# Totals of three groups interleaved with the next scores, and one more spatial unit as split products, in a retention and gated-MLP kernel

## The chip, the cores and the metric

The kernel runs on one core of a Trainium2 chip. The metric is device time in microseconds (us) of one execution, the median of several runs. The engines are TensorE (PE, with its weight loads as PEld), VectorE (DVE), ScalarE (ACT), GpSimd (POOL) and SyncE (SP), whose queue issues most loads.

## The reference

Retention with 4 batches, 8 heads, 768 positions and head size 64, then a gated MLP on its output:

```
state = gamma * state + k[t] (outer) v[t];  y[t] = scale * q[t] @ state      # per head
h = relu(x @ w_in);  u, v = halves of h                                      # x = y, 512 wide
v_n = (v - mean) / sqrt(var + 1e-6)
out = (u * (w_spatial @ v_n + b_spatial)) @ w_out
```

All inputs and the output are f32; w_spatial is 768 x 768, u and v are 512 wide.

## The kernel before

**Retention.** The sequence is cut into groups of 128 positions, six to a batch (24 groups g), each of two chunks i of 64 positions. For a chunk, 4 pairs of heads hp by 2 heads r are 64x64 matmuls. `place(hp, r)` names the half of the partitions on which head r of pair hp lies, so a matmul uses one quadrant of the 128x128 array: its rows are the half of its operands, its columns the half of its output. An f32 matmul stands as two records in the trace. For each group there are scores (k by q, tile `s`, masked by DVE into `scores`), a sum of k by v, and products with values and states (tile `x`), which give the output of the group.

**Two ways of the k by v sum.** In the steps S (`ret_set`), from group 6 on, scores of the next group and the k by v products of this one (tile `d`) are issued alternately, the latter into the opposite half of the output, and DVE (or ACT, line 369) brings them back to the right half while it adds the old state. In the opening, groups 0 to 5, `total_sum` (word t) adds the products into one standing PSUM tile `total`, and `total_copy` (word k, on ACT) copies it to the state; the next t waits for that copy.

**The MLP.** x is split in a high and a low part (`xh`, `xl`: words h and l after the evict E); v products (word V), u products (word u) and out products (word o) are fp32r products of three terms: high by high, high by low, low by high. A spatial unit (column block j, half of the positions) is `spatial_products`: six f32 products, or, where the half is the second and column j was split by `norm_split` (D), eighteen fp32r ones, with the spatial weights that `split_spatial` (W0 and W1) put in high and low parts by an ACT cast and a DVE residue for each of three blocks. A split column takes two of the four buffers tagged "ca", which the weight splits use before.

**The order.** The strings START, FIRST, REST and LAST are the program order, a word an action. In START every engine keeps that order. In FIRST and later PE keeps it, and other engines are ordered by a planner, but for W's casts and residues, which keep the program order too. In START the words c, H, R split w_in and w_out: c0, c1, c2 on DVE, H a cast on ACT, R the residue on POOL (R1 to R5) or DVE. p22 to p26 scale the values of groups 2 to 6 on ACT by eight multiplications each; j is the mask on DVE, q a block of scores, y01 the second chunk's x products of group 0. In FIRST, I4 is two blocks of u products, the spatial unit of column 0, second half, its gate, and an out product.

The lines that set the buffers:

```python
total[0] = ps_o.tile([P, NP, D], F32, tag="o", name="total")       # one tile for the whole run
return mpool.tile([P, 2, HC, P], dtype, tag="ca", name=name, bufs=4)
return ps_r.tile([P, 2, NP, C], F32, tag="ret", name=name)          # bufs=2: scores and d
```

Of the kernel before, what the change touches and what calls it, by code (L numbers as in the profile page):

```python
# [21 lines left out]


START = (
# [10 lines left out]
)  # L35
FIRST = (
    "S6 W0 I4 W1 D1 X6 J9 S7 G9 D2 I5 X7 J10 G10 D3 W2 S8 W3 I6 X8 S9 V0 G11 W4 I7 X9 J11 S10 "
    "G12 O7 N0 X10 W5 V1 V2 V3 N1 N2 J12 G13 S11 X11 J13 G14 V4 N3 S12 N4 V5 W6 N5"
)
REST = (  # L40
# [21 lines left out]
def tile_retention_gmlp(  # L62
# [12 lines left out]
    nc = tc.nc  # L75
    P = 128
    B = out.shape[0]
# [12 lines left out]
    ROWS = [slice(0, D), slice(D, P)]  # L90
# [27 lines left out]
    def keep(ins):  # L118

        if fixed:  # L120
            tc.keep_in_program_order(ins)

    def mm(out, lhs, rhs, start, stop, pin=False, shared=False):
        ins = nc.tensor.matmul(out, lhs, rhs, start=start, stop=stop, skip_group_check=shared)  # L124
        if pin or pinned or fixed:
            tc.keep_in_program_order(ins)
# [32 lines left out]
    def slot(n, dtype, name):  # L159

        cols = HALF // 2 if dtype == I64 else HALF
        return mpool.tile([P, HC, cols], dtype, tag=f"sp{n}", name=name, bufs=1)
# [5 lines left out]
    for n in ROOMS:  # L168
        t = slot(n, F32, f"room{n}").rearrange("p s c -> p (s c)")
# [85 lines left out]
    def place(hp, r):  # L255

        return ROWS[(r + hp) % 2]
# [40 lines left out]
    total = {}  # L298
    marks = {}

    def total_sum(g, i):
        if not total:
            total[0] = ps_o.tile([P, NP, D], F32, tag="o", name="total")
        for hp in range(NP):
            for r in range(2):
                rows = place(hp, r)
                mm(
                    total[0][rows, hp],
                    naturals[g][rows, i, hp],
                    values[g][rows, i, hp],  # L310
                    start=(g == 0 and i == 0 and hp == 0),
                    stop=True,
                    shared=True,
                )

    def total_copy(g, i):
        dst = states[g][:, 1] if i == 0 else states[g + 1][:, 0]
        keep(nc.scalar.copy(dst, total[0]))

    def score(g, i, hp, r, pin=False):  # L320
        rows = place(hp, r)
        ops = keys[g][rows, i, hp], queries[g][rows, i, hp]
        mm(marks[g][rows, i, hp], *ops, start=True, stop=True, pin=pin)

    def bank(name):
        return ps_r.tile([P, 2, NP, C], F32, tag="ret", name=name)
# [8 lines left out]
    def ret_mask(g):  # L335
        mk = mask_t[:, :].unsqueeze(1).broadcast_to([P, 2 * NP, C])
        s, d = (t.rearrange("p i h c -> p (i h) c") for t in (marks.pop(g), scores[g]))
        keep(nc.vector.tensor_tensor(d, s, mk, ALU.mult))
# [360 lines left out]
    def decay_copy():  # L699
# [17 lines left out]
        "q": lambda b, g, n: ret_scores(n),  # L717
        "p": lambda b, g, n: scale_values(n % 10, pick(n // 10)),
        "j": lambda b, g, n: ret_mask(n),
        "t": lambda b, g, n: total_sum(n // 10, n % 10),  # L720
        "k": lambda b, g, n: total_copy(n // 10, n % 10),
        "y": lambda b, g, n: out_products(n // 10, n % 10),
        "E": lambda b, g, n: out_evict(n),
# [114 lines left out]
```

## Time and profile before

| | |
|---|---|
| median of 3 runs | 373.97 us (372.93 to 374.14) |
| the profiled execution | 374.42 us, span 372.7 us |
| PE busy | 362.0 us (97%) |
| DVE, ACT, POOL busy | 237.2, 155.1, 135.5 us |
| granted TensorE clock | 1.00 |

The span is the time from the first to the last instruction of the profiled execution; its device time is 1.7 us longer. PE's matmuls are pipelined, so a busy PE need not be at its peak.

### The profile page before, as it was taken

How to read it: one execution, taken by the hardware profiler on the slowest of the kernel's cores; microseconds unless marked ns; L12 is line 12 of the kernel's file. 1: busy time of each engine (PE TensorE's matmuls, PEld its weight loads, DVE VectorE, ACT ScalarE, POOL GpSimd, SP SyncE). 2: the span in 40 equal slices, each digit the busy share in tenths (PEclk: the TensorE clock that was granted, in tenths of full speed). 3: DMA queues.
4: the chain of work that ended last, by engine and by line, in shares of the span. 5: the costliest groups of instructions: out<-in, count | busy, mean ns of one | idle time of the engine just before them, and what ended most of it. 6: DMA issues, size and time to landing. Idle time of an engine off the chain costs nothing.

```text
span 372.7 us, 10303 instructions
## 1 busy us (share of the span) xinstructions
PE 362.0 (97%) x4420; PEld 316.6 (85%) x4420; DVE 237.2 (64%) x514; ACT 155.1 (42%) x309; POOL 135.5 (36%) x137
## 2 busy tenths in 40 slices
PE   7798999999999999999999999999999999999995
PEld 3687785797998879999998888999998888999984
DVE  4989979995887866677674543376774433165530
ACT  3595781274334545533114445432323445432232
POOL 2254750001353523526424451327424341325041
PEclk9999999999999999999999999999999999999999
DMA  7997773001331731113305332021404002000022
GB/s 262 413 365 261 272 300 130 0 2 63 138 114 58 253 115 64 61 55 112 118 2 199 114 114 86 8 106 52 179 1 141 3 2 86 0 0 2 0 87 84
DMA packets 13153, 41.20 MB, mean 111 GB/s; under 512 B 1586, under 2 KB 1842, under 8 KB 13108
## 3 DMA queue, kind: packets, MB, share of 16 engines
q1 hardware_dynamic: 12964, 40.42, 29.8%
q8 instruction: 35, 0.57, 0.7%
q10 hardware_dynamic: 144, 0.13, 0.1%
q14 instruction: 10, 0.08, 0.1%
HBM read 34.25 MB, written 6.29 MB: 109 GB/s over the span
## 4 chain that ended last, share of the span: by engine, by line
PE 94%; DMA 2%; DVE 1%; issue 1%; ACT 0%; SPq 0%; POOL 0%; POOLq 0%; DVEq 0%
PE u L124 18%; PE v L124 18%; PE o L124 18%; PE y L124 10%; PE sp L124 8%; PE x L124 7%; PE z L124 5%; PE s L124 3%; PE d L124 3%; PE w L124 3%; DMA decay_t<-in_decay_dram 2%; PE total L124 1%; PE o_last L124 0%; SPq L129 0%; DVE xf L417 0%
## 5 line engine op out<-in xcount | busy, mean ns | idle before, releaser
L124 PE MATMUL u<-xh,winu_w 128*128 128x384 f32 x256 | 68.1, 338 | 0.0
L124 PE MATMUL v<-winv_w,xh 128*128 128x512 f32 x192 | 60.6, 397 | 0.0
L124 PE MATMUL o<-wout_w,gh 128*128 128x512 f32 (+1 forms) x192 | 60.4, 396 | 0.0
L124 PEld LDWEIGHTS u<-xh,winu_w 128*128 128x128 f32 x256 | 46.5, 188 | 0.8
L132 POOL TENSOR_TENSOR xl<-xf,xh 128x512 fp32r<-128x512 f32 x21 | 29.4, 1398 | 37.3 <-ACT xh L434 37.3
L124 PE MATMUL u<-xl,winu_w 128*128 128x384 f32 x128 | 42.9, 335 | 0.0
L124 PEld LDWEIGHTS v<-winv_w,xh 128*128 128x128 f32 x192 | 35.2, 188 | 7.8
L124 PE MATMUL y<-sp,a 128*128 128x384 f32 x216 | 41.6, 336 | 0.0
L124 PEld LDWEIGHTS o<-wout_w,gh 128*128 128x128 f32 x192 | 35.2, 188 | 7.3
L532 ACT CAST a<-vn 128x384 fp32r<-128x384 f32 x42 | 21.6, 514 | 46.0 <-PE y L124 16.9
L132 DVE TENSOR_TENSOR a<-vn,a 128x384 fp32r<-128x384 f32 x42 | 24.9, 593 | 24.6 <-ACT a L532 24.2
L132 POOL TENSOR_TENSOR gl<-ur,gh 128x384 fp32r<-128x384 f32 x24 | 26.8, 1116 | 37.4 <-ACT gh L628 37.0
L124 PEld LDWEIGHTS y<-sp,a 128*128 128x128 f32 x216 | 38.0, 188 | 0.2
L124 PE MATMUL v<-winv_w,xl 128*128 128x512 f32 x96 | 37.5, 390 | 0.0
L124 PE MATMUL o<-wout_w,gl 128*128 128x512 f32 (+1 forms) x96 | 37.3, 389 | 0.0
L475 DVE BATCH_NORM_STATS2 bst<-vr 128x6 f32<-128x512 f32 x24 | 16.6, 691 | 28.6 <-ACT vr L468 28.6
L417 DVE SCALAR_TENSOR_TENSOR xf<-x,decay_t,qd_t 128x128 f32<-128x128 f32 x96 | 27.1, 343 | 10.3 <-PE x L124 9.7
L482 POOL TENSOR_TENSOR rs<-rs,mhalf 128x1 f32<-128x1 f32 x24 | 13.5, 566 | 42.6 <-DVE rs L477 42.1
L124 PE MATMUL s<-qk 64*64 64x64 f32 x768 | 27.4, 221 | 0.1
L124 PEld LDWEIGHTS s<-qk 64*64 64x64 f32 x768 | 25.2, 137 | 2.1 <-issue 1.1
L498 ACT ACTIVATE vn<-vr,nb,rs 128x512 f32<-128x512 f32 x24 | 19.4, 814 | 17.8 <-DVE nb L487 16.8
L593 ACT ACTIVATE ur<-u 128x384 f32<-128x384 f32 x32 | 15.7, 490 | 26.8 <-PE u L124 26.6
(111 smaller groups left out, 671.7 us busy)
## 6 DMA issues: line engine op xcount, KB each, us to landing
qk<-in_groups_dram SPq DMA_DIRECT2D x24, 512.0 KB, 5.4
vk<-in_groups_dram SPq DMA_DIRECT2D x21, 512.0 KB, 4.8
out_dram<-ot SPq DMA_DIRECT2D x23, 256.0 KB, 2.9
wst<-in_w_sp_dram SPq DMA_DIRECT2D x4, 576.0 KB, 7.9
raw<-in_w_inv_dram SPq DMA_DIRECT2D x4, 512.0 KB, 7.3
raw<-in_w_inu_dram SPq DMA_DIRECT2D x4, 512.0 KB, 7.0
raw<-in_w_out_dram SPq DMA_DIRECT2D x4, 512.0 KB, 5.2
third<-in_groups_dram SPq DMA_DIRECT2D x3, 512.0 KB, 7.4
```

The costliest lines, as they stand in the source:

```text
L124: ins = nc.tensor.matmul(out, lhs, rhs, start=start, stop=stop, skip_group_check=shared)
L132: return eng.tensor_tensor(out, whole, high.bitcast(F32), ALU.subtract)
L417: nc.vector.scalar_tensor_tensor(xf[:, hp], t[hp % 2][:, hp // 2].rearrange("p i c -> p (i c)"), qg_t[:, c, hp : hp + 1], qd_t[:, hp], ALU ...
L475: keep(nc.vector.bn_stats(st, norm[b, c][0]))
L482: keep(nc.gpsimd.tensor_tensor(rs, rs, mhalf, ALU.pow))
L498: keep(nc.scalar.activation(vn[b][:, c], v, AF.Identity, bias=nb, scale=rs))
L532: nc.scalar.copy(t[:, 0], whole)
L593: keep(nc.scalar.activation(u, pu[:, :HALF], AF.Relu))
```

## The change

Three parts. In `total_sum` every product goes to the opposite half of the output, and for groups 2, 3 and 4 (words t120 to t141) each is issued right after a score product of the next group; the words q3, q4 and q5 are gone, and the masks j4 and j5 stand later, behind the second half of those scores. `total_copy` copies two halves instead of one whole, swapping them. In FIRST, W1 and a new D0 stand before I4, so that the spatial unit of column 0, second half, takes the split products.

```diff
 START, the parts that differ (before, after):
-... l0 H1 q3 t20 k20 E1 G4 R1 V00 j2 h1 t21 l11 p23 k21 y20 y21 L5 R2 j3 q4 t30 E2 a3 h2 j4 c30 V10 p24 ...
+... l0 H1 t120 k20 E1 G4 R1 V00 j2 h1 t121 l11 p23 k21 y20 y21 L5 R2 j3 t130 E2 a3 h2 c30 V10 p24 ...
-... V20 a5 k30 y30 c32 t31 H3 k31 c50 G5 y31 q5 E3 t40 a4 j5 R3 V21 V12 k40 c40 L6 c51 y40 p25 y41 t41 h3 ...
+... V20 a5 k30 y30 c32 t131 j4 H3 k31 c50 G5 y31 E3 t140 a4 R3 V21 V12 k40 c40 L6 c51 y40 p25 y41 t141 j5 h3 ...
 FIRST:
-    "S6 W0 I4 W1 D1 X6 J9 ...
+    "S6 W0 W1 D0 I4 D1 X6 J9 ...
-    def total_sum(g, i):
+    def total_sum(g, i, with_scores=False):
         if not total:
             total[0] = ps_o.tile([P, NP, D], F32, tag="o", name="total")
+        if with_scores and i == 0:
+            marks[g + 1] = bank(f"s{g + 1}")
         for hp in range(NP):
             for r in range(2):
-                rows = place(hp, r)
+                if with_scores:
+                    score(g + 1, i, hp, r)
+                rows, other = place(hp, r), place(hp, 1 - r)
                 mm(
-                    total[0][rows, hp],
+                    total[0][other, hp],
                     naturals[g][rows, i, hp],
                     values[g][rows, i, hp],
...
     def total_copy(g, i):
         dst = states[g][:, 1] if i == 0 else states[g + 1][:, 0]
-        keep(nc.scalar.copy(dst, total[0]))
+        for r in range(2):
+            keep(nc.scalar.copy(dst[ROWS[r]], total[0][ROWS[1 - r]]))
...
-        "t": lambda b, g, n: total_sum(n // 10, n % 10),
+        "t": lambda b, g, n: total_sum(n // 10 % 10, n % 10, n >= 100),
```

## Rows read from the trace of the kernel before

**Rows 1.** The page, busy us (share of the span) and instructions of PE.

```profile
PE 362.0 (97%) x4420; PEld 316.6 (85%) x4420; DVE 237.2 (64%) x514; ACT 155.1 (42%) x309; POOL 135.5 (36%) x137
```

**Rows 2.** Waits of PE, whole run: who waited for whom, total us, times, longest.

```profile
PE x L124 <- issue: 1.3, 2, 0.9
PE total L124 <- issue: 1.2, 1, 1.2
PE x L124 <- DVE ws L372: 0.2, 1, 0.2
```

**Rows 3.** Busy by stretch: length, busy us (instructions) by engine, clock, DMA share, GB/s.

```profile
16.90:27.40 10.50, 10.50 (x256) 9.17 (x252) 8.93 (x20) 9.81 (x34) 5.47 (x4) 1.00 0.99 370
22.80:41.15 18.35, 16.77 (x398) 14.08 (x392) 17.95 (x36) 13.24 (x39) 9.49 (x7) 1.00 0.77 267
```

**Rows 4.** Timeline of PE, merged: start us, length us, what, count.

```profile
17.48 1.97 PE L124 MATMUL s<-qk 64*64 64x64 f32 x62
...
19.35 0.63 PE L124 MATMUL total<-third 64*64 64x64 f32 x15
...
91.92 0.24 PE L124 MATMUL d<-vk 64*64 64x64 f32 x2
...
92.80 0.23 PE L124 MATMUL d<-vk 64*64 64x64 f32 x2
```

**Rows 5.** The chain that ended last, the two kinds of spatial unit.

```profile
85.27 3.87 PE sp L124 x12
...
95.34 3.12 PE sp L124 x18
```

**Rows 6.** Timeline of ACT: copies and the instruction behind them.

```profile
18.83 0.35 ACT L318 COPY third<-total 128x256 f32<-128x256 f32 x1
19.09 0.62 ACT L205 CAST winv_w<-df 128x512 fp32r<-128x512 f32 x1
...
81.17 0.74 ACT L369 COPY ws<-d 64x256 f32<-64x256 f32 x2
...
81.94 0.52 ACT L244 CAST sp<-wst 128x384 fp32r<-128x384 f32 x1
```

**Rows 7.** Timelines of POOL (R3) and DVE (c50, E3, c40, E5).

```profile
28.09 1.59 POOL L132 TENSOR_TENSOR df<-df,winv_w 128x512 f32<-128x512 f32 x1 [2.67 <-ACT winv_w L205]
29.76 1.33 POOL L212 TENSOR_TENSOR winv_w<-df,room 128x512 fp32r<-128x512 f32 x1
...
28.46 1.50 DVE L182 TENSOR_SCALAR room<-room 128x512 f32<-128x512 f32 x1
30.00 1.37 DVE L184 TENSOR_SCALAR room<-room 128x512 int32<-128x512 int32 x1
31.29 1.11 DVE L417 SCALAR_TENSOR_TENSOR xf<-x,decay_t,qd_t 128x128 f32<-128x128 f32 x4
...
33.37 0.43 DVE L184 TENSOR_SCALAR room<-room 128x512 int32<-128x512 int32 x1
...
41.47 1.12 DVE L417 SCALAR_TENSOR_TENSOR xf<-x,decay_t,qd_t 128x128 f32<-128x128 f32 x4 [0.32 <-PE x L124]
```

**Rows 8.** Busy by stretch from the start to two gaps; the page's instruction queue.

```profile
0.00:16.74 16.74, 11.78 (x223) 7.25 (x223) 11.08 (x23) 6.35 (x11) 4.93 (x14) 1.00 0.89 330
...
0.00:30.70 30.70, 25.66 (x603) 19.46 (x604) 23.40 (x45) 17.73 (x47) 12.94 (x20) 1.00 0.89 331
...
q8 instruction: 35, 0.57, 0.7%
```

**Rows 9.** Timelines of ACT (k50) and PE (y51, V30).

```profile
39.50 0.36 ACT L318 COPY third<-total 128x256 f32<-128x256 f32 x1
...
40.61 0.27 PE L124 MATMUL x<-third,third 64*64 64x64 f32 x3
...
41.28 0.73 PE L124 MATMUL v<-winv_w,xh 128*128 128x512 f32 x2
```

**Rows 10.** Timeline of DVE, the residues of W0.

```profile
84.45 1.49 DVE L132 TENSOR_TENSOR sp<-wst,sp 128x384 fp32r<-128x384 f32 x3
```

More of the change, by code (lines that the diff above doesn't have):

```diff
@@ L24 @@
 START = (
[10 rows of a table removed]
[10 rows of a table added]
 )
 FIRST = (
-    "S6 W0 I4 W1 D1 X6 J9 S7 G9 D2 I5 X7 J10 G10 D3 W2 S8 W3 I6 X8 S9 V0 G11 W4 I7 X9 J11 S10 "
+    "S6 W0 W1 D0 I4 D1 X6 J9 S7 G9 D2 I5 X7 J10 G10 D3 W2 S8 W3 I6 X8 S9 V0 G11 W4 I7 X9 J11 S10 "
     "G12 O7 N0 X10 W5 V1 V2 V3 N1 N2 J12 G13 S11 X11 J13 G14 V4 N3 S12 N4 V5 W6 N5"
```

20 rows, old and new, of the table START are left out of this document.

## Prediction, made before the changed kernel was run

> **What bounds the kernel now.** I read the page first. TensorE (PE) is busy 362.0 of 372.7 us [rows 1]: whatever shortens or delays it late in the run shows one for one. Then the waits of PE over the whole run. One of them, of 0.2 us behind DVE, comes after the first 41 us; the others fall before. Two of the early ones are named "issue", which is time in which PE waited for nothing that the profile shows [rows 2]. So a change after 41 us is worth its PE time; a change before must be traced to what PE waits for. Third, the busy time by stretch. From 16.90 to 27.40 us ScalarE (ACT) works 9.81 of 10.50 us, and from 22.80 to 41.15 us VectorE (DVE) works 17.95 of 18.35 us [rows 3]. PE only looks full there: the two engines that feed it have next to no room.
>
> **The change part by part.**
>
> *1. Scores and totals alternate (t120 to t141).* Before, a block of scores, or of totals, used only two of the four quadrants. The 62 score records at 17.48 took 1.97 us from first start to last end; less the 0.22 us of one record that is 28.7 ns each. Totals: (0.63 - 0.22) / 14 = 29 ns [rows 4]. The later steps S already alternate scores with products that write the opposite quadrant: from the first d pair at 91.92 to the last at 92.80 there are 15 steps of four records, 14.7 ns a record [rows 4]. Three groups have 32 score and 32 total records each: 192 x 14.0 ns = 2.7 us of PE. Its bounds are 0 (alternating does not pay here) and 2.7 us.
>
> The Trainium skill, TensorEngine Tiling, section Restrictions and Gotchas, says that different row tiles cannot use the same PSUM bank at the same time. By it the two score quadrants, which share a bank, would exclude each other, and the alternation would gain nothing. The 14.7 ns rows, same pattern and same banks, speak against it.
>
> *2. What this moves.* The scores of groups 3, 4 and 5 no longer run ahead of their totals. A total waits for its scaled values and for the copy of the total before it (it adds into the bank that the copy reads), and the scores now stand behind that wait on PE. So the 0.9 us that a score block used to cover such waits is gone: t120 waits for p22, t130 for p23 and k21, all on ACT. The masks j4 and j5 go behind c32 and c51 on DVE, with the same work.
>
> *3. The copy of the total is cut in two (k, 11 times).* Source and destination halves are swapped, so one 128x256 copy becomes two 64x256 ones. A whole copy let the next instruction start 0.26 us later (18.83 to 19.09). The nearest rows to a half copy are those of L369, the same form: two begin at 81.17 and the next instruction at 81.94, 0.385 us each with no overlap [rows 6]. A pair therefore costs 0.77 us, 0.50 us more than before. If half copies overlapped as the whole ones do, it would be 0.26 more. Four of them (k11, k20, k21, k30) lie between 16.9 and 27.4 us: 4 x 0.50 = 2.0 us, less the 0.69 us that ACT was idle there [rows 3] = 1.3 us; by the low price 1.04 - 0.69 = 0.35 us. I take the high price, since the row is of the same shape. So H3, the ACT cast behind k30, ends 0.35 to 1.3 us later.
>
> *4. Who waits for H3.* The residue R3 on GpSimd (POOL) starts on it at 28.09, and its two operations run to 31.09. In that time DVE's c50 needed 1.50 and 1.37 us for what takes 0.43 us undisturbed; E3 follows at 31.29 [rows 7]. With R3 late, E3 comes late by 0 to 1.3 us: 0 if c50 slips in ahead of, or between, R3's two operations, and all of it if c50 is held again. From E3 on DVE has no idle time until E5, which waited 0.32 us for PE [rows 7]; masks and splits are as many as before. E4 releases h4, H4, r2 and then k50 on ACT (39.50), now a pair, and k50 releases y51 and so V30 at 41.28 [rows 9]. Before, PE came to y51 at 40.61 us, after k50 had ended [rows 9]; PE, 2 us earlier by the alternation, will now wait for it. With E4 unmoved, the pair ends at 39.50 + 0.77 = 40.27, y51 takes 0.5 us, the turn to V30 0.25 us: V30 at 41.05 instead of 41.28, a gain of 0.23 us. With E4 later by 1.3 us: a loss of 1.1 us. I take the middle, slightly to the bad side, a loss of 0.5 us in START. The 2.7 us of PE then turn into waits at t120, t130 and y51.
>
> *5. The "issue" gaps.* One of 1.2 us stood in the middle of t40, after 603 matmuls; another after 223 [rows 2, 8]. The PE instructions (4420 + 4420, [rows 1]) over the 35 packets of the instruction queue [rows 8] make 253 a packet, 126 matmuls with their loads; the gaps lie 380 = 3 x 127 apart. So I read them as the instruction stream arriving late while the DMA engines are full. The instructions are the same in number, and the reordering puts the boundary 16 pairs further on, behind six V products that take 1.4 us. The gap may shrink from 1.2 to 0. I count it at nothing, because the DVE chain of part 4 ends after it.
>
> The Trainium skill, Runtime: NRT & Kernel Launch, section Instruction fetch mechanics, calls the cost of crossing a 16 KiB boundary mostly hidden. The 1.2 us gap disagrees, if it is one.
>
> *6. FIRST: column 0, second half.* 12 records of an f32 spatial unit took 3.87 us on the chain, the 18 of a split one 3.12 us [rows 5]: -0.75 us, on a PE with no idle time. To have it in time, D0 and W1 must be done early. D0 takes the pair of rooms, and the place on ACT and DVE, that D1 had, and D1 takes D2's; D2 now waits until the unit has read column 0, with some 15 us left. W1's three casts fit into ACT's idle time. Its three DVE residues come behind W0's, which ended at 84.45 + 1.49 = 85.94 [rows 10]: at 86.43, 86.93 and 87.43. The unit starts at 85.10 and needs them, at 0.52 us per pair of weights, at 86.84, 87.36 and 87.89. It fits with 0.4 us to spare. If another 0.95 us DVE operation goes between, the stall is 0.55 us. Bounds: 0.2 to 0.75 us; I take 0.75, since nothing ahead of them grows.
>
> **Sum.** The profiled execution took 374.42 us (span 372.7 and 1.7 around it), 0.45 above the median of the runs, 373.97. 374.42 + 0.5 - 0.75 = 374.2; against the median, **373.7 us**, within what a measurement of this kernel can tell from no change (0.3%, 1.1 us).
>
> **Rivals.**
>
> *PE sets START after all.* c50 or c51 escapes GpSimd (each hold is worth about 1 us on DVE), the half copies overlap, and the gap of part 5 closes. Then START gains 1.2 to 2.7 us, with part 6 1.9 to 3.4: 370.5 to 372.0. For it: holds on DVE depend on shifts of tenths. Against it: ACT's 9.81 of 10.50 us.
>
> *The copies win.* The k pairs put every scaling (p22 to p24) and cast behind them, by 0.5 us each. R3 and the later residue l3 are late and meet other DVE operations that they hold for one more us; START then loses 2 to 2.5 us, after part 6 1.3 to 1.8: 375.2 to 375.8. It decides from about 1.9 us of loss in START. For it: the DVE holds of rows 7; against it: only 2.0 us are added in the tight stretch, less 0.69 of idle.
>
> *Alternation does not pay for totals.* Scores and totals keep 28.7 ns, ACT is as in part 3: a loss of 1.3 us less 0.75: 374.5.
>
> *W1 late:* the 0.75 shrinks to 0.2: 374.3.
>
> **Numbers.** Forecast (START hidden under ACT and DVE, within 1.1 us) 0.48; PE sets START 0.29; copies win 0.15; no alternation 0.04; W1 late 0.04. Faster by over 0.3%: the second, and a little of the first: 0.32. Slower: the third, and a little of the rest: 0.17. Same: 0.51. The range reaches into both main rivals: 371.6 to 375.2. The likeliest case's own range is 372.9 to 374.9.
>
> **What would show it.** Part 1: 32 records of s and total in about 0.5 us. Part 3: the copies of the total in pairs 0.38 apart, ACT with hardly a gap from 17 to 28 us. Part 4: new PE waits at t120, t130 and y51, E3 and E4 between 0 and 1.3 us later. Part 6: 18 records of the split kind in 3.12 us where 12 stood, no wait before them. The prediction is wrong if V30 starts earlier than about 40.3 us or later than 42.8 us, or if the unit of column 0 waits for a residue.

## The result, and the profile after

The change made the kernel slower: 376.99 us (median of 6 runs, 376.61 to 377.75) against 373.98 (6 runs), a ratio of 1.0081, 95% interval 1.0060 to 1.0102. The forecast was 373.7, its range ended at 375.2. The profiled execution took 376.77 us, span 375.0 against 372.7.

The page first, its busy line of all engines and the row of TensorE's granted clock in forty slices:

```profile
PE 362.4 (97%) x4426; PEld 317.1 (85%) x4426; DVE 238.1 (63%) x515; ACT 161.4 (43%) x321; POOL 135.2 (36%) x137
...
PEclk9888999999999999999999999999999999999999
```

PE is 0.4 us busier than before [rows 1] and idle for 12.6 us instead of 10.7. That the alternation and the split products need less of its time does not show in its busy time, partly because the records of two stretches at a lower clock (below) are longer. ACT has 6.3 us more [rows 1] in 12 more instructions: eleven pairs of half copies by 0.50 are 5.5, and the cast of D0 is 0.83. The waits of PE, whole run (who waited for whom, total, times, longest), say where the idle time went [rows 2]:

```profile
PE total L124 <- issue: 3.1, 1, 3.1
PE total L124 <- ACT ws L323: 2.0, 2, 1.7
```

The timeline of PE places them (start, length, what, count, idle time before and its releaser):

```profile
15.80 0.51 PE L124 MATMUL total<-vk 64*64 64x64 f32 x10 [3.13 <-issue]
...
25.47 0.27 PE L124 MATMUL total<-vk 64*64 64x64 f32 x1 [1.66 <-ACT ws L323]
...
43.94 0.73 PE L124 MATMUL v<-winv_w,xh 128*128 128x512 f32 x2
...
87.84 3.70 PE L124 MATMUL sp<-sp,vn 128*128 128x384 f32 x18
```

The first row is t10. At 15.80 it starts when the pair k01 has ended (14.96 + 0.74), not for nothing as the name "issue" says. It waited for k01 before, too: at 14.07 the view names GpSimd's scaling, but that had ended at 13.18, and the whole copy k01 at 13.97. PE (t10), ACT (k01) and GpSimd before:

```profile
14.07 0.68 PE L124 MATMUL total<-vk 64*64 64x64 f32 x16 [1.54 <-POOL vk L296]
...
13.60 0.37 ACT L318 COPY ws<-total 128x256 f32<-128x256 f32 x1
...
12.14 1.04 POOL L296 TENSOR_TENSOR vk<-vk,decay_t 128x512 f32<-128x512 f32 x1 [2.78 <-DMA vk<-in_groups_dram]
```

The second row is t130, behind the pair k21 (24.67 + 0.74). The third is V30, 2.66 us later than before [rows 9]; the fourth the spatial unit of column 0.

**The span in four parts.** From V30 to that unit nothing depends on the change: 43.82 us before, 43.90 after, and 43.8 to 44.0 in the profile of every kernel below. From the group products x of X6, behind the unit and its out products, to the end it is 281.4 to 282.0 in all but one. So each span is the start of V30 + 43.9 + the stretch from the unit to X6 + 281.6. Before: 41.28 + 43.82 + 6.05 + 281.55 = 372.7. After: 43.94 + 43.90 + 5.70 + 281.46 = 375.0. START lost 2.66 us where a loss of 0.5 was forecast; FIRST gained 0.35 where 0.75 was.

ACT's timeline after shows p22, k21, H3 and k50 [rows 6, 9]:

```profile
17.72 2.02 ACT L293 ACTIVATE third<-third,decay_t 128x64 f32<-128x64 f32 x8
...
24.67 0.74 ACT L323 COPY ws<-total 64x256 f32<-64x256 f32 x2
...
30.00 0.62 ACT L205 CAST winv_w<-df 128x512 fp32r<-128x512 f32 x1
...
42.63 0.76 ACT L323 COPY third<-total 64x256 f32<-64x256 f32 x2
```

H3 is 2.61 us late; before it was:

```profile
27.39 0.62 ACT L205 CAST winv_w<-df 128x512 fp32r<-128x512 f32 x1
```

It adds up: p22 starts 0.81 us late (16.91 before); from p22 to H3 ACT is busy 11.88 of 12.28 us against 9.80 of 10.48, so 2.08 more work, of which idle time took only 0.28: 0.81 + 2.08 - 0.28 = 2.61.

DVE's timeline, first c20 and E0, then j4, c50, E3 and E4 [rows 7], then the residues [rows 10]:

```profile
11.56 0.43 DVE L182 TENSOR_SCALAR room<-room 128x512 f32<-128x512 f32 x1 [1.01 <-ACT room L176]
12.02 1.22 DVE L184 TENSOR_SCALAR room<-room 128x512 int32<-128x512 int32 x1
13.17 1.11 DVE L422 SCALAR_TENSOR_TENSOR xf<-x,decay_t,qd_t 128x128 f32<-128x128 f32 x4
...
32.54 0.69 DVE L343 TENSOR_TENSOR ws<-s,mask_t 128x512 f32<-128x512 f32 x1 [2.48 <-PE total L124]
33.15 0.47 DVE L182 TENSOR_SCALAR room<-room 128x512 f32<-128x512 f32 x1
33.65 0.43 DVE L184 TENSOR_SCALAR room<-room 128x512 int32<-128x512 int32 x1
33.99 1.12 DVE L422 SCALAR_TENSOR_TENSOR xf<-x,decay_t,qd_t 128x128 f32<-128x128 f32 x4
...
39.81 1.12 DVE L422 SCALAR_TENSOR_TENSOR xf<-x,decay_t,qd_t 128x128 f32<-128x128 f32 x4
...
87.10 2.42 DVE L132 TENSOR_TENSOR sp<-wst,sp 128x384 fp32r<-128x384 f32 x5
89.44 0.95 DVE L132 TENSOR_TENSOR vn<-vn,vn 128x768 fp32r<-128x768 f32 x1
90.31 0.55 DVE L132 TENSOR_TENSOR sp<-wst,sp 128x384 fp32r<-128x384 f32 x1
```

Three things are to be seen. At 12.02 an operation of c20 takes 1.22 us instead of 0.43 (11.58 to 12.01 before), while GpSimd scales group 1 from 11.92 to 12.96; before, c20 was done when that scaling began, at 12.14. At 32.54 DVE, which from 22.80 to 41.15 us had 0.4 us of idle time before [rows 3], waits 2.48 us: the mask j4 now stands behind t131, and c50 and E3 behind j4. E3 is 2.70 us late, and all of START's loss lies ahead of it. Not all of that is the mask's: E3 reads the products y31, which end on PE at 32.95 (row below) and ended at 29.28 before. So PE alone would have made E3 some 1.7 us late, and j4 and c50 ahead of it add 1.0. At 89.44 the residue of another column (D1) has slipped in ahead of W1's last. The end of y31 on PE:

```profile
32.65 0.30 PE L124 MATMUL x<-qk,ws 64*64 64x64 f32 x8
```

### The profile page after: what moved, and what is told of

It is laid out like the page before. It is cut to its first block, busy times and chain, and to the rows that moved or that the text cites. A ratio compares the mean times of both kernels' runs of the same rounds, so it can differ in the third digit from the quotient of the medians.

```text
span 375.0 us, 10330 instructions
## 1 busy us (share of the span) xinstructions
PE 362.4 (97%) x4426; PEld 317.1 (85%) x4426; DVE 238.1 (63%) x515; ACT 161.4 (43%) x321; POOL 135.2 (36%) x137
## 4 chain that ended last, share of the span: by engine, by line
PE 79%; DVE 10%; DMA 4%; issue 2%; ACT 2%; SPq 1%; POOL 0%; DVEq 0%; ACTq 0%
PE o L124 16%; PE v L124 15%; PE u L124 15%; PE y L124 10%; PE x L124 6%; PE z L124 5%; DMA vk<-in_groups_dram 4%; PE sp L124 3%; PE d L124 3%; PE w L124 2%; PE s L124 2%; DVE df L193 1%; SPq L129 1%; DVE df L132 1%; DVE room L202 1%
## 5 line engine op out<-in xcount | busy, mean ns | idle before, releaser
L124 PE MATMUL v<-winv_w,xh 128*128 128x512 f32 x192 | 61.7, 403 | 0.0
L132 DVE TENSOR_TENSOR a<-vn,a 128x384 fp32r<-128x384 f32 x42 | 25.9, 618 | 24.6 <-ACT a L537 24.2
L537 ACT CAST a<-vn 128x384 fp32r<-128x384 f32 x42 | 21.6, 514 | 46.1 <-PE y L124 16.9
L124 PE MATMUL s<-qk 64*64 64x64 f32 x768 | 28.9, 222 | 0.2 <-DMA qk<-in_groups_dram 0.2
L296 POOL TENSOR_TENSOR vk<-vk,decay_t 128x512 f32<-128x512 f32 x18 | 19.9, 1105 | 18.8 <-DMA vk<-in_groups_dram 10.8
```

The lines of the kernel that those rows point to most:

```text
L132: return eng.tensor_tensor(out, whole, high.bitcast(F32), ALU.subtract)
L296: tc.keep_in_program_order(engine.tensor_tensor(values[g], values[g], vd, ALU.mult))
L537: nc.scalar.copy(t[:, 0], whole)
```

## The experiments

V30 is the start in the profile (41.28 before); the ratio, with its 95% interval, is to runs of the kernel before on the same chip. One per cent is 3.7 us. Each kernel does all of the computation; e4 repeats some scores besides.

| kernel | V30 | time | ratio | interval |
|---|---|---|---|---|
| e1_first_only | 39.50 | 373.67 | 0.9975 | 0.9955 to 0.9996 |
| e2_halves_only | 42.98 | 375.20 | 1.0020 | 0.9997 to 1.0042 |
| e3_start_only | 43.88 | 376.66 | 1.0058 | 1.0038 to 1.0078 |
| e4_fill_second | 45.70 | 381.10 | 1.0174 | 1.0143 to 1.0205 |
| e5_order_only | 41.91 | 376.03 | 1.0035 | 1.0013 to 1.0057 |
| e6_halves_early | 41.65 | 375.92 | 1.0033 | 1.0013 to 1.0053 |
| e7_halves_mid | 41.30 | 373.67 | 0.9991 | 0.9972 to 1.0009 |
| e8_first_d1_late | 41.00 | 374.20 | 1.0000 | 0.9982 to 1.0017 |
| e9_c50_first | 41.77 | 375.77 | 1.0043 | 1.0015 to 1.0072 |
| e10_c50_dve | 43.24 | 375.41 | 1.0033 | 1.0018 to 1.0048 |
| e11_c50_dve_first | 42.93 | 375.76 | 1.0027 | 1.0004 to 1.0049 |
| e12_q4_back | 42.78 | 376.24 | 1.0042 | 1.0018 to 1.0067 |
| e13_order_c50 | 41.64 | 375.28 | 1.0023 | 1.0007 to 1.0039 |
| e14_early_k01 | 40.04 | 375.12 | 1.0018 | 0.9996 to 1.0039 |
| e15_first_pinned | 40.67 | 373.81 | 0.9989 | 0.9972 to 1.0006 |
| e16_all_mends | 41.94 | 374.28 | 0.9994 | 0.9970 to 1.0018 |
| e17_mends_q5 | 41.45 | 373.80 | 0.9984 | 0.9964 to 1.0005 |
| e18_k01_pinned | 40.61 | 374.07 | 1.0008 | 0.9988 to 1.0027 |

V30 and the time don't rank alike, because one profile is one execution: e1, e8, e15 and the kernel before have the same START, and V30 at 39.50, 41.00, 40.67 and 41.28. Sizes are therefore taken from the ratios, mechanisms from the profiles.

**The parts by themselves, and the clock.** The first theory was TensorE's clock: the changed kernel has two stretches below full speed. Its windows, whose columns are as in [rows 3]:

```profile
16.50:20.50 4.00, 4.00 (x108) 3.73 (x99) 3.90 (x10) 3.89 (x13) 0.00 (x0) 0.57 0.80 280
26.80:30.20 3.40, 3.40 (x10) 2.62 (x9) 3.16 (x6) 3.34 (x12) 0.13 (x1) 0.50 1.02 406
```

Before, both stretches had 1.00. In FIRST alone START is that of before; in the halves alone the totals go to the opposite half and are copied in halves, with order and FIRST of before; in START alone FIRST is that of before; the fourth kernel is the change with group 4's scores computed three times over (extra work on PE ahead of t130, to keep it busy).

```diff
 e1, on the kernel before:
-    "S6 W0 I4 W1 D1 X6 J9
+    "S6 W0 W1 D0 I4 D1 X6 J9
 e2, on the kernel before:
-                    total[0][rows, hp],
+                    total[0][other, hp],
...
-        keep(nc.scalar.copy(dst, total[0]))
+        for r in range(2):
+            keep(nc.scalar.copy(dst[ROWS[r]], total[0][ROWS[1 - r]]))
 e3, on the change:
-    "S6 W0 W1 D0 I4 D1 X6 J9
+    "S6 W0 I4 W1 D1 X6 J9
 e4, on the change (A42: the scores of group 4, twice):
-... R2 j3 t130 E2 ...
+... R2 j3 A42 t130 E2 ...
```

> Only the FIRST part of the change (W1 and D0 ahead of I4); START is that of before. Theory (the loss is made in START): 0.35 us below before if a residue of the second weight block comes late behind the residue of column 1, as in the changed kernel; 0.75 us if it is in time. Rival (the loss is made in FIRST, where the DVE work was pulled together): above before, by up to 2 us.

> Only the totals in the opposite half and the copy in two halves; START keeps the blocks of scores q3 to q5, nothing alternates, FIRST is that of before. Theory (a wait at t130 lets the granted clock fall, and the V products behind it run at half speed): the scores of group 4 stand between y21 and t30 and shorten the wait, the clock stays at 1.00 in the V products, and the loss is 0.5 to 1.2 us against before. Rival (the longer copies on ACT alone hold START back, whatever the clock): about 2.5 us above before.

> The whole START part of the change, FIRST as before. Theory and its rival on ACT alone: 2.6 to 2.8 us above before, with the clock at half in two stretches of the first 30 us. Rival (the loss is made in FIRST): within 0.5 us of before.

> The changed kernel with 1.9 us of idle repeats of the scores of group 4 on PE ahead of t130, in the place of its wait. Theory (the clock): the granted clock of V10 to V02 is 1.00, they take 3.3 instead of 5.2 us, and the time is 1.5 to 1.9 us below the changed kernel, about 375.2. Rival (ACT alone): the V products are faster, but what follows waits for ACT and DVE all the same, and the time is within 0.4 us of the changed kernel, 377.

The loss is START's: 0.58% (2.2 us) with FIRST as before. The halves alone, at 1.0020, can't be told from 1. The low clock of the second stretch isn't needed for the loss: in START alone that stretch has full clock,

```profile
26.80:30.20 3.40, 3.40 (x46) 2.60 (x48) 3.14 (x6) 3.34 (x12) 0.11 (x1) 1.00 0.99 398
```

and V30 is at 43.88, as after. t131 comes earlier there, j4 at 30.93 instead of 32.54, but then R3 on GpSimd (30.68) catches c50 and holds one of its operations for 1.40 us: E3 at 33.59 instead of 33.99. Here PE is not what holds E3, since y31 ends at 31.34; the other 2.25 us are c50, behind j4 and beside R3. DVE, then R3's second operation, then y31:

```profile
30.93 0.69 DVE L343 TENSOR_TENSOR ws<-s,mask_t 128x512 f32<-128x512 f32 x1 [0.88 <-PE total L124]
...
32.27 1.40 DVE L184 TENSOR_SCALAR room<-room 128x512 int32<-128x512 int32 x1
33.59 1.11 DVE L422 SCALAR_TENSOR_TENSOR xf<-x,decay_t,qd_t 128x128 f32<-128x128 f32 x4
...
32.02 1.35 POOL L212 TENSOR_TENSOR winv_w<-df,room 128x512 fp32r<-128x512 f32 x1
...
31.04 0.30 PE L124 MATMUL x<-qk,ws 64*64 64x64 f32 x8
```

The fill proved nothing by itself: the extra scores met a gap of their own, 1.96 us put down to "issue", the clock fell all the same (0.64), and j4 came at 33.90.

This does not rule out the clock altogether. The first stretch is below full speed in START alone, too (0.67), and over many runs the time goes with the clock: of 138 runs of the kernel before that stand beside these experiments, the 81 with a mean granted clock of 0.997 or more had a median of 374.01 us, the 43 from 0.993 to 0.996 had 374.73, and the 14 below that 375.76. The change's six runs had 0.988 to 0.994. So the clock may make a part of the loss. It does not make all of it: at like clocks and on the same chip, the order alone (e5, below) took 375.01 against 374.10 us (6 and 18 runs at 0.997 or more), and the early half copies (e6) 375.99 against 374.52 (11 and 13 runs from 0.993 to 0.996).

**Order, early copies and middle copies apart.** Each on the kernel before, with totals in their old quadrants: the order of START alone, whole copies; then the first three copies in halves (k00, k01, k10); then the four of the prediction's part 3.

```diff
 e5: START of the change; total[0][rows, hp]; keep(nc.scalar.copy(dst, total[0]))
 e6 and e7, in total_copy:
+        if (g, i) in ((0, 0), (0, 1), (1, 0)):              # e6
+        if (g, i) in ((1, 1), (2, 0), (2, 1), (3, 0)):      # e7
+            for r in range(2):
+                keep(nc.scalar.copy(dst[ROWS[r]], total[0][ROWS[r]]))
```

> The kernel before with the order of the change alone: the scores of groups 3 to 5 alternate with the totals and the masks j4 and j5 stand later, but the totals stay in their old half, so the copies are whole and the alternation uses the same two quadrants as the scores. FIRST is that of before. Theory (the ACT work of the halved copies sets START back): H3 on ACT starts at 27.4 to 28.0 us as before, and the time is within 0.6 us of before. Rival (the scores that no longer cover PE's waits cost time by themselves, as the step from the second to the third run, 1.4 us, lets one think): 1.2 to 2 us above before.

> The kernel before with the first three copies of the total (k00, k01, k10) in two halves, without a swap of the halves; nothing else changed. Theory (each pair adds 0.5 us to the chain k00, a2, c20, E0, h0, k01, t10, k10, p22 on ACT and DVE, and c20 meets the scaling of group 1 on POOL): p22 starts 0.8 us later than at 16.9, and the time is 0.2 to 0.9 us above before. Rival (only the tight stretch from 17 to 28 us counts; the start waits for a transfer anyway): within 0.2 us of before. If the swap of halves is what makes a half copy hold up the next instruction, a pair takes 0.64 us here instead of 0.77.

> The kernel before with the copies k11, k20, k21 and k30 in two halves, without a swap; nothing else changed. Theory: ACT has 0.7 us of idle time against 2.0 us more work between 16.9 and 27.4 us, H3 starts 1.3 to 1.6 us later than at 27.4, and the time is 0.8 to 1.4 us above before. Rival (the early copies are what counts): within 0.3 us of before.

The order costs 0.35%, the early copies 0.33% (1.3 and 1.2 us), the middle ones nothing. That last is the surprise: H3 is at 30.14, later than after. DVE and GpSimd in e7:

```profile
29.90 0.42 DVE L182 TENSOR_SCALAR room<-room 128x512 f32<-128x512 f32 x1
30.36 0.43 DVE L184 TENSOR_SCALAR room<-room 128x512 int32<-128x512 int32 x1
31.46 1.13 DVE L421 SCALAR_TENSOR_TENSOR xf<-x,decay_t,qd_t 128x128 f32<-128x128 f32 x4 [0.67 <-PE x L124]
```

```profile
30.84 1.27 POOL L132 TENSOR_TENSOR df<-df,winv_w 128x512 f32<-128x512 f32 x1 [5.14 <-ACT winv_w L205]
```

With R3 as late as 30.84, c50 is done before it, in 0.42 and 0.43 us instead of 1.50 and 1.37, and E3 moves by 0.17 us only. A late H3 is harmless as long as c50 need not wait. In the order alone it must wait, for j4. DVE in e5, j4, c50 and E3:

```profile
30.13 0.69 DVE L342 TENSOR_TENSOR ws<-s,mask_t 128x512 f32<-128x512 f32 x1 [1.80 <-PE total L124]
30.74 0.79 DVE L182 TENSOR_SCALAR room<-room 128x512 f32<-128x512 f32 x1
...
31.91 1.12 DVE L421 SCALAR_TENSOR_TENSOR xf<-x,decay_t,qd_t 128x128 f32<-128x128 f32 x4
```

In e6 a second question was answered too: its halves don't swap sides and still take 0.74 to 0.76 us a pair, so the price is that of the half copy, not of the swap.

**c50 ahead of j4.**

```diff
 e9 on START alone, e13 on the order alone:
-... c32 t131 j4 H3 k31 c50 G5 ...
+... c32 t131 H3 k31 c50 j4 G5 ...
```

> The START part of the change with one word moved: the split step c50 stands ahead of the mask j4 on DVE instead of behind it; FIRST as before. Theory (j4 now waits on DVE for t131 on PE, and c50 behind it then meets R3 on GpSimd): c50 runs right behind c32, ahead of R3, E3 starts 1 us or more earlier than at 33.6 us, and the time falls by 0.8 to 1.5 us against the third run, to about 375.4. Rival (the late ACT chain sets E3 and E4, whatever stands where on DVE): within 0.4 us of the third run, 376.7.

> The order of the change with the quadrants, whole copies and FIRST of before, and c50 on DVE ahead of the mask j4. Theory (j4 waits for t131 on DVE and so pushes c50 into R3 on GpSimd, which holds it): c50 runs before R3 starts, in some 0.45 us an operation, E3 starts near 31.0 instead of 31.9, V30 near 41.0 instead of 41.9, and the time comes 0.8 to 1.2 us below that of the same kernel with j4 first, to 0 to 0.4 us above before. Rival (the order costs because the scores stand behind PE's waits, whatever DVE does): E3 may be early but V30 stays near 41.9 and the time 1.0 to 1.6 us above before.

DVE in e13, c50, j4, E3 and j5:

```profile
28.24 0.43 DVE L182 TENSOR_SCALAR room<-room 128x512 f32<-128x512 f32 x1
28.71 0.43 DVE L184 TENSOR_SCALAR room<-room 128x512 int32<-128x512 int32 x1
30.56 0.69 DVE L342 TENSOR_TENSOR ws<-s,mask_t 128x512 f32<-128x512 f32 x1 [1.43 <-PE total L124]
31.17 1.12 DVE L421 SCALAR_TENSOR_TENSOR xf<-x,decay_t,qd_t 128x128 f32<-128x128 f32 x4
...
36.22 0.69 DVE L342 TENSOR_TENSOR third<-s,mask_t 128x512 f32<-128x512 f32 x1 [2.08 <-PE total L124]
```

c50 is free and E3 0.74 us earlier than in e5, as the theory has it. But V30, at 41.64, is nearer to the rival's 41.9 than to the theory's 41.0, and the ratio falls from 1.0035 to 1.0023 only, and in START alone from 1.0058 to 1.0043, both within the intervals. So the times don't show that the swap of c50 and j4 helps by itself. In e13's profile the second moved mask, j5, waits 2.08 us for t141 and takes back what E3 gained (E4 at 37.89 against 37.45 in e5).

**Other places of the early halves and of group 4's scores.** e10 is e9 with the second halves of k00, k01 and k10 on DVE, and R20 before k00; e11 adds FIRST; e12 is START alone with group 4's scores as a block (q4) and j4 at their old place.

```diff
 e10, in total_copy, and in START (e11 with FIRST of the change):
+            copy = nc.vector.tensor_copy if r and (g, i) in EARLY_COPIES else nc.scalar.copy
+            keep(copy(dst[ROWS[r]], total[0][ROWS[1 - r]]))
-... t00 k00 y00 y01 t01 R20 G1 ...
+... t00 R20 k00 y00 y01 t01 G1 ...
 e12:
-... j3 t130 E2 a3 h2 c30 ... c32 t131 j4 H3 ...
+... j3 q4 t30 E2 a3 h2 j4 c30 ... c32 t31 H3 ...
```

> The ninth run's kernel, and the second halves of the first three copies (k00, k01, k10) on DVE instead of ACT, with R20 written ahead of k00. Theory (two things hold START back, the early pairs on ACT, 1.2 us by the sixth run, and the mask j4): a2 starts 0.4 us earlier, c20 misses the scaling on GpSimd, t10 starts at about 14.3 us instead of 15.8, and the time is another 0.6 to 1.2 us below the ninth run, about 374.5. Rival (three more operations on DVE cost what ACT saves): no better than the ninth run.

> The tenth run's kernel and the FIRST part of the change: the whole change, mended. Theory: 0.3 us below the tenth run, within 0.8 us of before. If PE set START now, 1.9 to 3.4 us below before.

> The START part of the change with the middle group undone: the scores of group 4 as a block q4 ahead of t30 again and the mask j4 back ahead of c30, groups 3 and 5 still alternate; totals in the opposite half, copies in two; FIRST as before. Theory (j4 behind t131 is what the alternation costs): the time falls from the third run's 376.7 to that of the second, 375.2, or a little below. Rival (any score block taken from PE's waits costs alike): about a third of the way, 376.2.

All three lie within the interval of e9 and show little. In e10 t10 came at 14.51, about as forecast, but the work on DVE made a new wait, 1.5 us of the chunk after t10 for the mask j1. In e12 E3 came early (31.80), E4 at 38.65: j5 again.

**k01 ahead of h0.** In e6 the cast h0 waits for E0, E0 for c20, c20 for a2 and a2 for the pair k00; k01 stood behind h0, with its total long ready.

```diff
-... E0 q1 h0 k01 c21 j1 ...
+... E0 q1 k01 h0 c21 j1 ...
```

> The first three copies of the total in halves, as in the run before that cost 1.2 us, but the copy k01 stands ahead of the cast h0 on ACT, in time in which ACT had waited for that cast's input. Theory (the early halves cost because they stand in the chain of ACT that ends in t10): t10 waits for GpSimd's scaling alone, as before or less (about 14.0 or earlier instead of 15.07), V30 at most 41.3, and the time within 0.4 us of before. Rival (the halves cost by their work, wherever they stand, or by a later link such as c20): t10 stays near 15.0, and the time 0.8 to 1.6 us above before.

PE and DVE in e14: t10 and the chunk behind it; c20's second operation and the mask j1:

```profile
13.02 0.68 PE L124 MATMUL total<-vk 64*64 64x64 f32 x16 [0.22 <-POOL vk L296]
16.00 0.34 PE L124 MATMUL x<-ws,vk 64*64 64x64 f32 x8 [2.30 <-DVE ws L342]
```

```profile
11.99 1.26 DVE L184 TENSOR_SCALAR room<-room 128x512 int32<-128x512 int32 x1
...
15.26 0.68 DVE L342 TENSOR_TENSOR ws<-s,mask_t 128x512 f32<-128x512 f32 x1
```

t10 comes 2 us earlier than in e6 (15.07), so its wait was ACT's. The other link stays: GpSimd's scaling holds c20, j1 is 1.16 us later than before (14.10), and the next chunk waits for it. The ratio, 1.0018, can't tell theory from rival.

**FIRST: what delays W1's last residue.** e1 and e8 (D1 further on in the program), e15 (D1's residue kept behind W1's on DVE), e18 (e15 with the whole copy k01 ahead of h0).

```diff
 e8:
-    "S6 W0 W1 D0 I4 D1 X6 J9 S7
+    "S6 W0 W1 D0 I4 X6 J9 D1 S7
 e15 and e18, in norm_split:
-        keep(residue(nc.vector, low, whole, high))
+        ins = residue(nc.vector, low, whole, high)
+        tc.keep_in_program_order(ins) if j == 1 else keep(ins)
```

> The FIRST part alone, with D1 written behind X6 and J9, so that its residue cannot go between the residues of W1; START is that of before. Theory (the unit of column 0 waited for the last residue of W1, behind that of column 1): the 18 split records follow each other without a wait, 3.1 us, and the time is 0.7 to 0.8 us below before, 0.3 to 0.4 below the first run. Rival (the residues are late with or without D1, by the work of S6 ahead of them): no better than the first run.

> The change in FIRST alone, with the residue of D1 on DVE kept in program order, behind W1's three. Theory (D1's residue, 0.95 us, is what slips in ahead of W1's last): the six residues of W0 and W1 follow one another, the spatial unit of column 0 has its 18 records without a gap in 3.1 us, and the time is 0.6 to 0.8 us below before, some 0.35 below the change in FIRST alone. Rival (something else holds the last residue, or the late residue of D1 makes the unit of column 1 wait): a gap stays ahead of the last pair of records or opens ahead of column 1, and the time is 0.2 to 0.45 below before.

> The kernel before with the change in FIRST, the residue of D1 pinned behind W1's, and the whole copy k01 ahead of h0; nothing else of the change. Theory (FIRST is worth 0.7 once D1's residue is out of the way, and t10 waited for more than GpSimd's scaling): t10 starts near 13.2 instead of 14.07, the mask j1 then holds the next products a little, V30 comes 0 to 0.5 us earlier, and the time is 0.5 to 1.1 us below before. Rival (the run of FIRST with the residue pinned, 0.33 us below, was its true worth, and t10 is not on the chain): the time is 0.1 to 0.5 us below before.

e8 didn't move what it meant to: in it, too, the planner put D1's residue ahead of W1's last one (86.95, then 87.82). The profiles of all kernels together settle it. "Lead" is how long before the unit DVE begins the residues of W0 and W1; the stretch is from the unit to X6. In the other kernels with the new FIRST the lead is 0.2 us with the START of before (e8, e18) and 0.6 to 0.8 with that of the change or a mended one (e4, e11, e17):

| kernel | residues from | unit from | lead | D1's residue between | stretch |
|---|---|---|---|---|---|
| before (f32 unit, 12 records) | 84.45 | 85.10 | 0.65 | none needed | 6.05 |
| e1 | 83.08 | 83.33 | 0.25 | yes | 6.23 |
| after | 87.10 | 87.84 | 0.74 | yes | 5.70 |
| e15 | 84.33 | 84.54 | 0.21 | no | 5.66 |
| e16 | 85.11 | 85.84 | 0.73 | no | 5.29 |

Both matter: half a microsecond of lead is worth 0.4 to 0.5 us, D1's residue out of the way 0.4 to 0.6, and only with both is the gain the 0.76 us of the unit's own time. The same shows in the rows of e15 and e16, residues and unit:

```profile
84.33 2.90 DVE L132 TENSOR_TENSOR sp<-wst,sp 128x384 fp32r<-128x384 f32 x6
```

```profile
85.84 3.28 PE L124 MATMUL sp<-sp,vn 128*128 128x384 f32 x18
88.96 0.62 PE L124 MATMUL o<-wout_w,gh 128*128 128x512 f32 x2
```

The last pair's residue ends at 87.23 in e15, where the unit began at 84.54 and could have been done by 87.66; its out products start at 88.03. In e16 they start 3.12 us after the unit. In e1 the unit's stretch is 0.18 us longer than before: FIRST alone, on the START of before, gained nothing there. In its profile e1 was faster by START's V30 at 39.50, and e8, with the same START and nearly the same stretch (6.22), did not repeat its 0.25%. e18 had one later wait for a load (1.4 us) in its profile, and no gain.

**All mends together.** e16 is the whole change with k01 ahead of h0, c50 ahead of j4 and D1's residue pinned; e17 also takes group 5's scores back to a block, with j5 where it was.

```diff
 e17, on e16:
-... j4 G5 y31 E3 t140 a4 R3 V21 ... y41 t141 j5 h3 ...
+... j4 G5 y31 q5 E3 t40 a4 j5 R3 V21 ... y41 t41 h3 ...
```

> The whole change with three mends: k01 ahead of h0 on ACT, c50 ahead of j4 on DVE, the residue of D1 behind those of W1. Theory (these three places are where the change loses): START loses 0 to 0.5 us, FIRST gains 0.7, and the time is 0.2 to 0.7 us below before. Rival (the half copies from 17 to 28 us and the waits of the scores cost by themselves what the mends do not touch): H3 stays near 30, V30 near 42.5, and the time is 0.3 to 1.3 us above before.

> The change with the three mends, and besides group 5's scores as one block (q5) ahead of E3, its mask j5 behind t40 as before, and t40 and t41 without scores; the alternation is left for groups 2 and 3. Theory (behind t141, the mask j5 keeps DVE waiting, 0.9 us in the order alone and 2.1 us with c50 first, and so E4 with all that follows): j5 runs without a wait, E4 starts at 37.0 or earlier instead of 37.8, V30 near 41.0, and the time is 0.5 to 1.2 us below before. Rival (PE's half microsecond a chunk of plain scores comes back as a loss, or c51 is held instead): E4 stays at 37.5 to 38.0 and the time within 0.4 us of before.

Two words moved and one residue pinned take the change from 1.0081 to 0.9994, and the intervals lie apart. In e16's profile START still loses 0.66 us, and FIRST gains the 0.76. By the ratios that is more than the two moves did alone (e13 against e5, e14 against e6), though the intervals leave room. A reason that fits the profiles, but is not shown, is that they act on one chain, ACT to t10, PE to t131, DVE to E3. In e17 j5 no longer waits; DVE, j5 and E4:

```profile
31.66 0.68 DVE L343 TENSOR_TENSOR third<-s,mask_t 128x512 f32<-128x512 f32 x1
...
35.64 1.13 DVE L422 SCALAR_TENSOR_TENSOR xf<-x,decay_t,qd_t 128x128 f32<-128x128 f32 x4 [0.37 <-PE x L124]
```

E4 is 2.18 us earlier than in e16 (37.82), but V30 only 0.49 (41.45): PE now has gaps of 1.0 and 0.5 us put down to "issue", and E5 waits 0.76 us for PE. Its ratio, 0.9984, reaches across 1. Of all versions only e1 has an interval below 1, and e8 and e15, with the same START and a FIRST as good or better, don't bear it out.

## Why the prediction was wrong

**Parts 1 and 5 were right in their numbers.** 32 records of scores and totals take half a microsecond (t120, from 20.57), and the time saved became waits, as said. The Trainium skill, TensorEngine Tiling (Array Packing), section Restrictions and Gotchas, says that two row tiles can't use one PSUM bank at the same time. The prediction inferred from it that the alternation would gain nothing, and saw the rule contradicted. The trace doesn't contradict it: in t120 the 16 records of the total, which share a bank, start 31 ns apart on average (20.57 to 21.04), about as in a block of totals (29 ns), and the scores between them go to another bank. The gaps named "issue" in [rows 2] are gone after (the one of that name is t10's wait for k01), and V30 is late all the same. A third gap before, of 0.39 us at 39.39, stood after 729 matmuls, 126 behind the second, which fits part 5's reading of them; no run tested it.

**Two terms were put at nothing, and these are the steps that failed: the early copies in part 3 and the order in part 2.** Alone they cost 0.33% (e6) and 0.35% (e5), together 2.5 us, where START alone lost 2.2 us by its ratio and the forecast had 0.5. With the halves in it the order costs about as much as alone: START alone (e3) lies 0.38% above the halves alone (e2).

**Part 3 was right in its price and wrong in its count.** A pair costs 0.76 us as forecast, and four pairs between p22 and H3 added 2.08 us, against 4 x 0.50. But "less the 0.69 us that ACT was idle there" gave back 0.28 only; part of that idle time was ACT's own wait for PE and DVE. And the sum left out the three pairs ahead of 16.9 us, which made t10 1.73 and p22 0.81 us late. H3 came 2.61 us late instead of 0.35 to 1.3. The four pairs that were counted cost no time in e7, on the order of before; on the new order all eleven pairs add 0.23% (e3 against e5).

**Part 2:** "The masks j4 and j5 go behind c32 and c51 on DVE, with the same work." The work is the same, but a mask behind t131 waits for everything ahead of t131 on PE, and DVE, with 0.4 us to spare in that stretch, keeps strict order: c50 and E3 queue behind it. j4 waits 2.48 us after, 1.80 in the order alone, 0.88 in START alone, and 0.24 with c50 first and the early chain mended (e16: E3 at 31.15, against 33.99 after and 31.29 before). The wait is not E3's loss one for one: after, 1.0 us of E3's 2.70 is j4 and c50 and the rest is the late y31; in START alone E3 stands 2.25 us behind y31. That the order costs time is measured (e5); that j4 is how, and j5 after it, is read from the profiles.

**Part 4 had the right stations and half of the link.** R3's hold on c50 is real (1.40 us in START alone), and the bound "0 if c50 slips in ahead" came true in e7. A late H3 and R3 by themselves cost nothing there; they meet c50 when j4 has made it late as well. (The terms for V30 with E4 unmoved add up to 41.02, not 41.05.) Two of the prediction's own signs came: V30 at 43.94, later than 42.8, and a unit that waits for a residue.

**Part 6 was mis-sized: 0.35 us instead of 0.75.** "If another 0.95 us DVE operation goes between, the stall is 0.55 us" is what happened, with D1's residue; it was named and not taken. With the residue pinned, e16 shows the 0.76. The lead of the residues over the unit, 0.65 us before, was taken as fixed; with the new FIRST on the START of before it is 0.2 us, and why is not shown.

**The rivals.** "The copies win" gave the nearest time, 375.2 to 375.8 with a START loss of 2 to 2.5, and had 0.15. Its route, the four middle pairs and a longer hold by R3, isn't what happened: e7 made those pairs and lost nothing, and no hold by R3 grew: c50 lost 2.0 us to it before and 1.2 in START alone.

**Open.** How START's 2.66 us divide exactly: the early copies cost 1.2 us by their ratio and 0.4 in their profile, and the order 1.3, each alone. What the clock costs was not separated from the waits that go with it.

## What to carry to other kernels

An instruction that is moved "with the same work" is to be priced by what it now waits for and by what queues behind it: on an engine in strict order without idle time, a mask that waits 2 us holds up its queue for 2 us, and that is lost unless the queue would have waited for the same engine anyway. Here two swaps of independent words and a pinned residue together gave the loss back; one swap alone stayed within the noise. When work is cut in halves or a copy grows, count every instance, also those outside the tight stretch, and don't set idle time off against it if that idle time is itself a wait for another engine. A residue that is just in time needs its order pinned, or the planner may put something else there.

## What the runs showed of the hardware

A copy of 64 partitions by 256 takes 0.38 us of ACT and overlaps with nothing, where the whole 128x256 lets the next instruction start after 0.26 us (e6: 0.74 to 0.76 a pair, with or without a change of side). Half a copy holds ACT longer than a whole one, 0.38 us against 0.26.

After the change TensorE's granted clock fell where PE had waited longer than before: to 0.57 in 4.0 us after 3.13 us at t10, and to 0.50 in 3.4 us after 1.66 us at t130. In the second stretch pairs of v products that take 0.62 us took 1.05, so the level there is 1.2 GHz. The wait alone doesn't settle it: in e16 t130 waited 1.66 us too, and that stretch had 1.00; in e7 t10 waited 1.55 us, as before (1.54), and the first stretch had 0.60 instead of 1.00. In START alone the second stretch kept its clock, and V30 came at the same time (43.88 against 43.94).

DVE's second operation of c20 took 1.22 us instead of 0.43 beside GpSimd's scaling of group 1 (e14: 1.26, e16: 1.18), so 0.44 us of delay by ACT (c20 at 11.56 against 11.12) became 1.25 us at E0 (13.17 against 11.92).
